# The second mixer's channel products by Strassen's seven block products, on a float32 attention and two-mixer kernel

## The chip, the cores and the metric

The kernel runs on one core of one Trainium2 chip. The metric is the time of one execution on the device in microseconds (us), the median of several executions; lower is better.

## What is computed

Clustered attention (a query sees the keys whose nearest centroid is its own), then two mixers on the result, all in float32. The part that matters here is the second mixer, and in it the channel part, the last two lines:

```python
def _moe2_ref(x, w_tok1, w_tok2, w_ch1, w_ch2) -> np.ndarray:
    xt = x.transpose(0, 2, 1)
    h = np.maximum(xt @ w_tok1, 0.0) @ w_tok2
    u = x + h.transpose(0, 2, 1)
    h2 = np.maximum(u @ w_ch1, 0.0) @ w_ch2
    return (u + h2).astype(np.float32)
```

Here x is 2 batches of 768 tokens by 512 channels, the token part goes through 256 columns, the channel part through 1536. The first mixer has the same channel part with 2048 columns. Weights arrive as 64-bit floats.

## The kernel before

TensorE runs float32 products in its fp32r form, which keeps fewer bits than float32. So every factor is split in two, a rounded high part and the rest, and each product takes three matmuls: high by high, high by low, low by high. A helper `mm` on line 73 issues every matmul of the products, so all have this line; `rnd` (L78, ScalarE) makes a high part, `sub` (L85, VectorE or GpSimd) the low part.

The program is written out by hand in Python loops, so every engine executes exactly the order in which the code records its instructions. It has four stretches.

1. Attention: 96 tile steps. ScalarE, VectorE and TensorE work in turn.
2. The first mixer's channel part. Tokens go in 3 passes of 512 columns (2 batches of 768 tokens make 1536), hidden columns in 16 blocks of 128, so 48 units. A unit is `hidden` (12 matmuls of 512 columns into bank 4 or 5), its eviction `hidden_out` (ScalarE takes the ReLU as `gh`, then VectorE makes `gl`), and `outmm` (12 matmuls of 512 columns into banks 0 to 3). The generator `half_slots` alternates them: `hidden(k+1)`, then `outmm(k)`. Each 12 matmuls are called a half slot here; 96 of them make this stretch.
3. The second mixer's token part, `tok(b)` for each batch: 6 times 4 transposes (L874), 36 matmuls of 512 columns, 48 of 384, in 20 pieces, of which one goes between two half slots.
4. The second mixer's channel part: the same `hidden` and `outmm` over 3 passes and 12 blocks, 36 units.

Beside the half slots runs the conversion of the weights from 64 bits (`conv`: one ScalarE instruction, L96, then four on VectorE, L100, L103, L106, L109), the split in high and low (L78, and L85 on GpSimd), and a write to a DRAM scratch (`scr_a` for the first mixer, `scr_b` for the second). The second mixer's weights go through it in 24 blocks of 512 columns, one every second half slot from the 40th on (`narrow`, `tick`). In the third pass of the first mixer and in the whole of the second, `feed` loads each unit's weights back from the scratch, two transfers of 512 KB per unit, into three rotating buffers; they are asked for some two units ahead. All of these transfers are issued by SyncE, in program order, to one hardware queue.

VectorE also adds the residual back together (L796, high plus low part), once per pass and mixer, and adds the products to it (L801).

## Time and profile before

| | |
|---|---|
| median of 3 runs | 752.43 us (751.09 to 754.22) |
| span of the profiled execution | 754.4 us |
| TensorE busy | 742.3 us (98%), 3902 matmuls recorded |
| VectorE busy | 467.4 us (62%) |
| ScalarE busy | 312.8 us (41%) |
| GpSimd busy | 169.8 us (23%) |
| TensorE clock granted, mean | 0.997 of full speed |

The profile was taken of one execution. For that execution the page gives the span from the first to the last instruction and no separate time; the span lies 0.2 us above the longest of the three runs. Matmuls overlap in the pipeline, so how long one costs is read from the distance between starts of neighbours, not from its duration.

### The profile page before, as it was taken

To read this page: it belongs to the slowest core of one execution; us is meant where nothing else is said; L and a number is where in the kernel's file an instruction comes from. 1 tells how busy PE (TensorE), PEld (TensorE's weight loads), DVE (VectorE), ACT (ScalarE), POOL (GpSimd) and SP (SyncE) were. 2 spreads that over 40 slices of the span, in tenths; PEclk is the share of its full clock that TensorE was granted. 3 is DMA by queue.
4 is the path that set the end of the run, shared out by engine and by line. 5 is a ranking of instruction groups with operands and counts; after the bars stand their busy time and mean duration, and the time that the engine had idled before them with its cause. 6 is when DMAs were issued, how large, how long until landed. Compare 5 with 4: busy or idle time off the path is not lost.

```text
span 754.4 us, 10584 instructions
## 1 busy us (share of the span) xinstructions
PE 742.3 (98%) x3902; PEld 589.3 (78%) x3902; DVE 467.4 (62%) x695; ACT 312.8 (41%) x568; POOL 169.8 (23%) x149
## 2 busy tenths in 40 slices
...
GB/s 179 189 195 220 139 190 214 220 209 131 71 37 124 121 181 195 215 201 189 177 111 128 245 369 358 314 238 280 260 318 204 201 113 293 194 190 206 238 190 84
DMA packets 51555, 149.60 MB, mean 198 GB/s; under 512 B 7696, under 2 KB 15760, under 8 KB 49456
## 3 DMA queue, kind: packets, MB, share of 16 engines
...
q14 instruction: 20, 0.16, 0.1%
...
## 4 chain that ended last, share of the span: by engine, by line
PE 94%; DMA 1%; DVE 1%; ACT 1%; SPq 1%; issue 0%; POOL 0%; ACTq 0%; POOLq 0%; DVEq 0%
PE ps L73 83%; PE ps L319 8%; DMA qk<-pt 1%; DMA sq__81<-in_qT_dram 1%; PE ps L874 1%; PE ps L382 1%; PE ps L339 1%; PE ps L405 0%; ACT p L302 0%; DVE nm L297 0%; POOL qk L85 0%; SPq L257 0%; SPq L268 0%; ACT pt L78 0%; DVE am L219 0%
## 5 line engine op out<-in xcount | busy, mean ns | idle before, releaser
L778 DVE SCALAR_TENSOR_TENSOR gl<-ps,gh 128x512 fp32r<-128x512 f32 x84 | 58.0, 691 | 209.6 <-ACT gh L777 209.6
L777 ACT ACTIVATE gh<-ps 128x512 fp32r<-128x512 f32 x84 | 50.2, 598 | 312.8 <-PE ps L73 312.8
L73 PE MATMUL ps<-gh,qk 128*128 128x512 f32 x544 | 179.6, 391 | 0.1
L73 PEld LDWEIGHTS ps<-gh,qk 128*128 128x128 f32 x544 | 102.1, 188 | 21.6 <-issue 0.5
L73 PE MATMUL ps<-qk 112*128 112x384 f32 (+2 forms) x456 | 109.7, 367 | 5.3 <-ACT p L302 4.0
L297 DVE TENSOR_REDUCE nm<-ps 128x1 f32<-128x768 f32 x96 | 91.2, 954 | 30.6 <-PE ps L73 29.3
L73 PE MATMUL ps<-gl,qk 128*128 128x512 f32 x272 | 106.0, 390 | 0.0
L85 POOL TENSOR_TENSOR qk<-c__77,qk 128x512 fp32r<-128x512 f32 x40 | 54.9, 1380 | 190.7 <-ACT qk L78 162.8
L302 ACT ACTIVATE p<-ps,nm 128x768 f32<-128x768 f32 x96 | 86.1, 899 | 22.8 <-DVE nm L297 20.7
L319 PEld LDWEIGHTS ps<-ident,p 128*128 128x128 f32 x576 | 69.1, 142 | 32.8 <-issue 26.9
L319 PE MATMUL ps<-ident,p 128*128 128x128 f32 x576 | 91.9, 279 | 0.4 <-DVE pt L324 0.3
L73 PEld LDWEIGHTS ps<-qk 112*128 112x128 f32 (+1 forms) x456 | 76.9, 191 | 13.5 <-ACT p L302 7.6
L73 PE MATMUL ps<-u2h,qk 128*128 128x512 f32 x224 | 73.9, 391 | 0.0
L73 PE MATMUL ps<-pt,vr 128*64 128x384 f32 x384 | 72.1, 498 | 0.0
L326 ACT COPY pt<-ps 128x512 f32<-128x512 f32 x96 | 55.7, 586 | 28.0 <-PE ps L319 25.1
L73 PEld LDWEIGHTS ps<-gl,qk 128*128 128x128 f32 x272 | 51.1, 188 | 10.2
L73 PE MATMUL ps<-u1h,qk 128*128 128x512 f32 x160 | 52.6, 390 | 0.0
L73 PEld LDWEIGHTS ps<-u2h,qk 128*128 128x128 f32 x224 | 42.1, 188 | 8.6
L100 DVE TENSOR_SCALAR c__77<-c__77 128x512 f32<-128x512 f32 (+2 forms) x47 | 47.7, 1015 | 0.8 <-ACT c__77 L96 0.7
L109 DVE SCALAR_TENSOR_TENSOR c__77<-c__76,c__77 128x512 int32<-128x512 int32 (+2 forms) x47 | 43.4, 924 | 1.5
L106 DVE SCALAR_TENSOR_TENSOR c__77<-c__76,c__77 128x512 int32<-128x512 int32 (+2 forms) x47 | 43.5, 925 | 1.1
L73 PE MATMUL ps<-u2l,qk 128*128 128x512 f32 x112 | 43.6, 390 | 0.0
...
## 6 DMA issues: line engine op xcount, KB each, us to landing
qk<-scr_b SPq DMA_DIRECT2D x72, 512.0 KB, 4.2
...
qk<-scr_a SPq DMA_DIRECT2D x32, 512.0 KB, 7.4
c__76<-in_wb_dram SPq DMA_DIRECT2D x24, 512.0 KB, 5.3
scr_b<-qk SPq DMA_DIRECT2D x24, 512.0 KB, 5.0
scr_a<-wx SPq DMA_DIRECT2D x16, 512.0 KB, 3.3
scr_a<-qk SPq DMA_DIRECT2D x16, 512.0 KB, 3.2
...
```

The lines of the kernel that those rows point to most:

```text
L73: pe.matmul(o, lhsT=l, rhs=r, start=start, stop=stop, **kw)
L85: eng.tensor_tensor(out=o, in0=a, in1=b, op=ALU.subtract)
L100: dve.tensor_scalar(out=dst, in0=dst, scalar1=2.0 ** -15, scalar2=122879.9921875, op0=ALU.max, op1=ALU.min)
L106: dve.scalar_tensor_tensor(out=d, in0=lo, scalar=29, in1=d, op0=ALU.logical_shift_right, op1=ALU.bitwise_or)
L109: dve.scalar_tensor_tensor(out=d, in0=hi, scalar=-0x40000000, in1=d, op0=ALU.bitwise_and, op1=ALU.bitwise_or)
L297: dve.tensor_reduce(out=nm[:, n % 4 : n % 4 + 1], in_=ps[:, b0 : b0 + 2, 0:HS], axis=AX.XY, op=ALU.max, negate=True)
L302: act.activation(p32[n % NP32].rearrange("p (j k) -> p j k", j=2), ps[:, b0 : b0 + 2, 0:HS], AF.Exp, bias=nm[:, n % 4 : n % 4 + 1], accum_ ...
L319: pe.transpose(ps[:, tb[j], ts(i, P)], p32[n % NP32][:, ts(c, P)], ident)
L326: act.copy(o, ps[:, tb[j], :])
L339: pe.transpose(ps[:, bk, ts(t, P)], osb[q % 2][:, ts(t, P)], ident)
L777: act.activation(gh, o, AF.Relu)
L778: dve.scalar_tensor_tensor(out=gl, in0=o, scalar=0.0, in1=f32(gh), op0=ALU.max, op1=ALU.subtract)
```

## The change

The last stretch is rewritten by the method of Strassen (in Winograd's form, which shares sums). A product of two matrices cut in 2 by 2 blocks needs seven block products in place of eight, if sums of the blocks are formed first and sums of the products afterwards. Both channel products of the second mixer are done so. For the first, tokens of a batch are halved (384 each), channels are halved, and two hidden blocks form a pair; for the second likewise.

- Weight sums: `quad` takes the place of `narrow` for these weights. One quad converts 1024 columns (two hidden blocks, one of the two weights), forms the four sums on VectorE, splits seven blocks of 256 columns (VectorE now subtracts for four of them, GpSimd for three) and writes 3584 columns to `scr_b` by two transfers, 768 KB and 1024 KB. There are 12, placed by the table `line` at half slots 54 to 92, with steps from four before to three after.
- Token sums: `build_u` forms the seven operands of a batch from the mixer's input, in tiles of 768 columns.
- Products: `h_mm` is one of the seven for the first weight, 6 matmuls of 384 columns, `h_out` its eviction and the sums and ReLUs that come after it; `o_mm` is one of the seven for the second weight, for one half of its rows, also 6 matmuls of 384 columns, `o_out` its addition to the result. A run is a batch and two pairs: 14 products of each kind. In the loop the products of the next run's first weight alternate with those of this run's second weight; those of the first run alternate with the pieces of `tok(1)`.
- Buffers: `turn_over` gives the conversion's buffers up for a ring of weights at half slot 93. `load1` and `load2` fetch weights by 256 to 1024 KB.
- The residual: `umm_out` lets ScalarE copy the transposed input back to `xn`, and the additions on L796 are gone.

```diff
-    scr = {0: dp.tile([NFA, 2, P, 1024], F32, name="scr_a"), 1: dp.tile([NFB, 2, P, 1024], F32, name="scr_b")}
+    NPR = NFB // 2
+    scr = dp.tile([NFA, 2, P, 1024], F32, name="scr_a")
+    scr2 = dp.tile([NPR, 2, P, 7 * 512], F32, name="scr_b")
...
-        return [lambda: rnd(act, uh, o), lambda: sub(dve, ul, o, f32(uh))]
+        return [lambda: rnd(act, uh, o), lambda: sub(dve, ul, o, f32(uh)), lambda: act.copy(xn[:, b, :, t, :], o)]
...
+    def quad(q, d, n):
+
+        pr, w = divmod(q, 2)
+        r64, r32 = w64[n % 2], w32[n % 2]
+        ops = conv(r32, r64)
+        r = r32.rearrange("p (i n) -> p i n", n=256)
+        i12 = 1 + w
+        r11, r12, r21, r22 = r[:, 0, :], r[:, i12, :], r[:, 3 - i12, :], r[:, 3, :]
+        A, B = stA[2 if q == 2 * NPR - 1 else q % 2], stB[q % 2]
+        raw_, hi_ = s32, f32(B[:, :, 0, :])
+        if d == 1:
+            raw_load(r64.rearrange("p (f n) -> p f n", f=2), wb[2 * pr : 2 * pr + 2, :, ts(w, 512)].rearrange("f p n -> p f n"))
+        elif d < 6:
+            ops[{3: 0, 4: 1, 4.5: 2, 5: 3, 5.5: 4}[d]]()
+        elif d == 6:
+            sub(dve, raw_[:, 3, :], r11, r21)
+            sub(dve, raw_[:, 1, :], r22, raw_[:, 3, :])
+            sub(dve, raw_[:, 2, :], r12, raw_[:, 1, :])
+            dve.scalar_tensor_tensor(out=raw_[:, 0, :], in0=r21, scalar=-1.0, in1=r22, op0=ALU.mult, op1=ALU.subtract)
+        elif d == 7:
+            rnd(act, A[:, 0, 0, :], r11)
+            rnd(act, A[:, 1:3, 0, :], r[:, i12 : 4 : 3 - i12, :])
+            rnd(act, B[:, :, 0, :], raw_)
+            sub(pool, A[:, 0, 1, :], r11, f32(A[:, 0, 0, :]))
+            sub(pool, A[:, 1:3, 1, :], r[:, i12 : 4 : 3 - i12, :], f32(A[:, 1:3, 0, :]))
+        elif d == 7.5:
+            sub(dve, B[:, :, 1, :], raw_, hi_)
+        elif d == 8:
+            sp.dma_start(scr2[pr, w, :, 0:1536], f32(A).rearrange("p i h n -> p (i h n)"))
+            sp.dma_start(scr2[pr, w, :, 1536:3584], f32(B).rearrange("p i h n -> p (i h n)"))
...
-        uh, ul = fst["u"][p]
-        if lo == 0 and f == hi - 3:
-
-            for b, s, n, k in pieces(p * TW, TW):
-                for c in range(NC):
-                    dve.tensor_tensor(out=x2[b][:, c, s : s + n], in0=f32(uh[:, c, k : k + n]), in1=f32(ul[:, c, k : k + n]), op=ALU.add)
...
+    line = [(wide, 6, 10), (wide, 7, 15), (wide, 8, 17), (wide, 9, 20), (wide, 10, 23), (wide, 11, 26), (wide, 12, 29), (mixer, 0, 33),
+            (wide, 13, 37), (wide, 14, 40), (wide, 15, 43), (mixer, 1, 46), (mixer, 2, 48), (mixer, 3, 50)]
+    line += [(quad, q, h) for q, h in enumerate((54, 59, 62, 65, 69, 72, 75, 79, 82, 85, 89, 92))]
+    for n, (f, k, h) in enumerate(line, 6):
+        steps = [(h - 4, (3,)), (h - 3, (4, 4.5)), (h - 2, (5, 5.5))]
+        if f is quad:
+            steps += [(h - 1, (6,)), (h, (7,)), (h + 1, (7.5,)), (h + 3, (8,))]
+        else:
+            steps += [(h, (6, 6.5)), (h + 1, (7,))]
+        if n > 7:
+            steps.append((line[n - 8][2] - 1, (1,)))
+        for s, ds in steps:
...
+    ORDER = (1, 5, 6, 3, 7, 2, 4)
+    PLACE = (0, 3, 4, 5, 6, 1, 2)
+    CHUNKS = ((0, 1), (1, 2), (3, 2), (5, 2))
+    HB = ((4, 5), (0, 1))
+    OB2 = ((2, 3), (6, 7))
+    NG = NPR // 2
+    CHAIN = (0, 1, 0, 1, 0, 1, 0)
+    FRESH = (True, True, False, False, False, True, False)
...
+    def build_u(b):
+
+        B = {(i, j): x2[b][:, 2 * i : 2 * i + 2, ts(j, HS)] for i in range(2) for j in range(2)}
+        o = {i: ops_u[b][pos(i)] for i in ORDER}
+        hi = lambda i: o[i][:, 0]
+        lo = lambda i: o[i][:, 1]
+
+        def flat(i, x):
+            return [lambda: rnd(act, hi(i), x), lambda: sub(pool, lo(i), x, f32(hi(i)))]
+
+        t = [fz[:, 768 * i : 768 * i + 768].rearrange("p (c n) -> p c n", c=2) for i in range(2)]
+
+        def cut(i, x, eng=pool):
+            return [lambda: rnd(act, hi(i), x), lambda: sub(eng, lo(i), x, f32(hi(i)))]
+
+        def add(o, x, y, op):
+            return [lambda: dve.tensor_tensor(out=o, in0=x, in1=y, op=op)]
+
+        return (flat(1, B[0, 0]) + add(t[0], B[0, 0], B[0, 1], ALU.subtract) + cut(5, t[0], dve) + add(t[1], B[1, 1], t[0], ALU.add)
+                + cut(6, t[1], dve) + add(t[0], B[1, 0], t[1], ALU.subtract) + flat(3, B[1, 1])
+                + add(t[1], B[1, 1], B[0, 1], ALU.subtract) + cut(7, t[1]) + flat(2, B[1, 0]) + cut(4, t[0], dve))
+
...
+    def turn_over():
+
+        cp_ctx.close()
+        op = ctx.enter_context(tc.tile_pool(name="op", bufs=1, side="right"))
+        ring_ = op.tile([P, 4096], F32R, name="ring")
+        mid_ = op.tile([P, 5 * HS], F32, name="mid")
+        w1b.extend([ring_[:, ts(i, 1024)] for i in range(4)] + [wx_[:, 3072:4096]])
+        tmps.extend([mid_[:, ts(i, HS)] for i in range(5)] + [fz[:, 1536 + HS * i : 1536 + HS * i + HS] for i in range(2)])
+
...
+    runs = [(b, k) for b in range(NB) for k in range(NG)]
+    seq1 = [(b, 2 * k + i, c) for b, k in runs for i in range(2) for c in range(4)]
+    seq2 = [(b, k, c) for b, k in runs for c in range(4)]
+    at1, at2 = {}, {}
+
+    def load1(n):
+        if n < len(seq1):
+            b, pr, c = seq1[n]
+            s, m = CHUNKS[c]
+            x = w1b[n % len(w1b)][:, 0 : 512 * m]
+            sp.dma_start(f32(x), scr2[pr, 0, :, 512 * PLACE[s] : 512 * (PLACE[s] + m)])
+            for i in range(m):
+                at1[b, pr, s + i] = x[:, ts(i, 512)].rearrange("p (h n) -> p h n", h=2), n, i == m - 1
+
+    def load2(n):
+        if n < len(seq2):
+            b, k, c = seq2[n]
+            s, m = CHUNKS[c]
+            x = w2b[n % len(w2b)][:, 0 : 1024 * m].rearrange("p (r n) -> p r n", r=2)
+            sp.dma_start(f32(x), scr2[2 * k : 2 * k + 2, 1, :, 512 * PLACE[s] : 512 * (PLACE[s] + m)].rearrange("r p n -> p r n"))
+            for i in range(m):
+                at2[b, k, s + i] = x[:, :, ts(i, 512)].rearrange("p r (h n) -> p r h n", h=2), n, i == m - 1
+
...
+    def h_mm(b, pr, s):
+        w, n, ends = at1[b, pr, s]
+        u = ops_u[b][s]
+        o, on = ps[:, HB[pr % 2][CHAIN[s]], 0:HS], dict(skip_group_check=not FRESH[s])
+        for c in range(2):
+            cs = ts(c, P)
+            mm(o, w[:, 0, cs], u[:, 0, c, :], c == 0 and FRESH[s], False, **on)
+            mm(o, w[:, 0, cs], u[:, 1, c, :], False, False, **on)
+            mm(o, w[:, 1, cs], u[:, 0, c, :], False, c == 1, **on)
+        if ends:
+            load1(n + len(w1b))
+
+    def h_out(b, pr, s):
+        x = ps[:, HB[pr % 2][CHAIN[s]], 0:HS]
+        g = gs.setdefault((b, pr), {})
+        hi, lo = (lambda i: g[i][:, 0, :]), (lambda i: g[i][:, 1, :])
...
+        if s == 0:
+            held_[1] = tmp()
+            act.copy(held_[1], x)
+        elif s == 1:
+            held_[3] = tmp()
+            act.copy(held_[3], x)
+        elif s == 2:
+            held_[0] = tmp()
+            act.copy(held_[0], x)
+        elif s == 3:
+            dve.tensor_tensor(out=held_[0], in0=x, in1=held_[0], op=ALU.add)
+            act.activation(held_[0], held_[0], AF.Relu)
+        elif s == 4:
+            new(3, 7)
+            held_[7] = tmp()
+            dve.tensor_tensor(out=held_[3], in0=x, in1=held_[3], op=ALU.add)
+            top(3, held_[3])
+            relu_less(held_[7], held_[3], held_[0], ALU.subtract)
+            cut(7, held_[7])
...
+    def o_mm(b, k, s, j):
+        w, n, ends = at2[b, k, s]
+        o, on = ps[:, OB2[j][CHAIN[s]], 0:HS], dict(skip_group_check=not FRESH[s])
+        for i in range(2):
+            g = gs[b, 2 * k + i][ORDER[s]]
+            wh, wl = (w[:, i, h, ts(j, P)] for h in range(2))
+            mm(o, wh, g[:, 0, :], i == 0 and FRESH[s], False, **on)
+            mm(o, wh, g[:, 1, :], False, False, **on)
+            mm(o, wl, g[:, 0, :], False, i == 1, **on)
+        if j:
+            gfree.extend(gs[b, 2 * k + i].pop(ORDER[s]) for i in range(2))
+            if ends:
+                load2(n + len(w2b))
+
...
-    while done < end(0, 2) - 24:
+    while done < 68:
         for t in bg:
             next(t, None)
         advance(done + 1)
-    drain(tok(0), end(0, 2) - 2)
-    advance(end(0, 2))
-    drain(tok(1), end(1, 0) - 2)
-    for _ in gen:
+    drain(tok(0), END - 2)
+    todo = build_u(0)
+    while done < END:
+        next(bg[1], None)
+        for _ in range(3):
+            if todo:
+                todo.pop(0)()
+        if done == END - 3:
+            for t in bg:
+                for _ in t:
+                    pass
+            turn_over()
+            for n in range(len(w1b)):
+                load1(n)
+        advance(done + 1)
+    for f in todo:
+        f()
+
+    t = tok(1)
+    for i in range(14):
+        pr, s = divmod(i, 7)
+        h_mm(0, pr, s)
+        h_out(0, pr, s)
+        for _ in range(1 + (1 <= i < 9) if i else 0):
+            next(t, None)
+        if i == 9:
+            load2(0)
+    for _ in t:
         pass
+    for n in range(1, len(w2b)):
+        load2(n)
+    todo = []
+    for r, (b, k) in enumerate(runs):
+        nxt = runs[r + 1] if r + 1 < len(runs) else None
+        if (b, k) == (0, 0):
+            todo = build_u(1)
+        for i in range(14):
+            if nxt:
+                pr, s = divmod(i, 7)
+                pr += 2 * nxt[1]
+                h_mm(nxt[0], pr, s)
+            s_, j = divmod(i, 2)
+            o_mm(b, k, s_, j)
+            if nxt:
+                for x in {6: (), 7: (6, 7)}.get(i, (i,)):
+                    h_out(nxt[0], 2 * nxt[1] + x // 7, x % 7)
+            o_out(b, k, s_, j)
+            send(2 if nxt else 0)
+            for _ in range(int(r == 0 and 4 < i) + 2 * int(r == 1 and i > 7)):
+                if todo and (r == 1 or len(todo) > 9):
+                    todo.pop(0)()
+    send(0)
```

Three places in the order of instructions follow. The first is SyncE's queue in the third pass of the first mixer, before (c is the conversion's buffer, qk the weights' buffer, scr_a and scr_b the scratches):

```order
L593 DMA scr_b<-qk_73 128x1024
L574 DMA c__76<-in_wb_dram 128x512
L757 DMA qk_73<-scr_a 128x1024
L757 DMA qk_72<-scr_a 128x1024
L593 DMA scr_b<-qk_73 128x1024
L574 DMA c__76<-in_wb_dram 128x512
L757 DMA qk_73<-scr_a 128x1024 x2
```

and the same pass now (c holds two blocks per transfer):

```order
L617 DMA scr_b<-vz 128x1536
L618 DMA scr_b<-qk 128x2048
L766 DMA qk<-scr_a 128x1024 x3
L617 DMA scr_b<-qk 128x1536
L618 DMA scr_b<-qk 128x2048
L535 DMA c__77<-in_wb_dram 128x2x512
L766 DMA qk<-scr_a 128x1024 x3
L535 DMA c__77<-in_wb_dram 128x2x512
L766 DMA qk<-scr_a 128x1024
```

A write of 512 KB ahead of every two weight loads has become a pair of writes of 1792 KB ahead of every three or four.

The second is VectorE in that pass, between the evictions `gl` of two units, before:

```order
L778 SCALAR_TENSOR_TENSOR gl_2308<-ps,gh_2306 128x512
L100 TENSOR_SCALAR c__77<-c__77 128x512
L103 TENSOR_SCALAR c__77<-c__77 128x512
L106 SCALAR_TENSOR_TENSOR c__77<-c__76,c__77 128x512
L109 SCALAR_TENSOR_TENSOR c__77<-c__76,c__77 128x512
L778 SCALAR_TENSOR_TENSOR gl_2309<-ps,gh_2307 128x512
```

and now (the eviction is L787, its output lies in the tile ug; fz holds the sums):

```order
L787 SCALAR_TENSOR_TENSOR ug<-ps,ug 128x512
L100 TENSOR_SCALAR c__78<-c__78 128x1024
L103 TENSOR_SCALAR c__78<-c__78 128x1024
L85 TENSOR_TENSOR qk<-fz,qk 128x4x256
L106 SCALAR_TENSOR_TENSOR c__78<-c__77,c__78 128x1024
L109 SCALAR_TENSOR_TENSOR c__78<-c__77,c__78 128x1024
L787 SCALAR_TENSOR_TENSOR ug<-ps,ug 128x512
L85 TENSOR_TENSOR fz<-c__78 128x256
L85 TENSOR_TENSOR fz<-c__78,fz 128x256 x2
L607 SCALAR_TENSOR_TENSOR fz<-c__78 128x256
```

Between two evictions stand twice the columns, and instructions of a new kind, the sums and a subtraction of 1024 columns.

The third is TensorE where the second mixer's channel part begins, now (ring and wx hold weights; u, wx, qk and vz the token sums; L878 are transposes of `tok(1)`, its matmuls read ug and tt):

```order
L73 MATMUL ps<-u_2310,ring 128x384 x12
L878 MATMUL ps<-ident,xn 128x128 x8
L73 MATMUL ps<-u_2310,ring 128x384 x6
L878 MATMUL ps<-ident,xn 128x128 x8
L73 MATMUL ps<-wx,ring 128x384 x6
L878 MATMUL ps<-ident,xn 128x128 x8
L73 MATMUL ps<-wx,ring 128x384 x6
L73 MATMUL ps<-ug,tt 128x512 x12
L73 MATMUL ps<-qk,ring 128x384 x6
```

Before, a piece of `tok(1)` stood between two half slots of 12 matmuls; here two pieces stand between two products of 6.

## Rows read from the trace of the kernel before

**Rows 1.** The page's head.

```profile
span 754.4 us, 10584 instructions
```

**Rows 2.** Stretches: length, busy us (instructions) PE, PEld, DVE, ACT, POOL; clock, DMA share, GB/s.

```profile
200.00:230.00 30.00, 30.00 (x200) 21.98 (x197) 24.55 (x36) 23.18 (x46) 3.18 (x3) 1.00 0.26 80
230.00:425.00 195.00, 195.00 (x953) 157.80 (x952) 132.33 (x188) 67.91 (x106) 45.22 (x34) 1.00 0.45 162
425.00:475.00 50.00, 49.89 (x232) 40.93 (x231) 38.12 (x57) 16.64 (x30) 10.45 (x9) 1.00 0.98 358
475.00:525.00 50.00, 50.00 (x231) 42.64 (x230) 30.27 (x42) 15.91 (x32) 17.21 (x16) 1.00 0.79 266
```

**Rows 3.** The chain that ended last, from 230 us on, by line.

```profile
by line: PE ps L73 96.6%; PE ps L874 1.0%; PE ps L319 0.9%; PE ps L382 0.7%; PE ps L339 0.2%; DVE xn L801 0.1%; issue 0.0%
```

**Rows 4.** TensorE's timeline, 512- and 384-column matmuls: start us, us, what.

```profile
494.24 0.39 PE L73 MATMUL ps<-gl,qk 128*128 128x512 f32 x1
...
494.92 0.39 PE L73 MATMUL ps<-gl,qk 128*128 128x512 f32 x1
...
496.05 0.33 PE L73 MATMUL ps<-t2h,yh 128*128 128x384 f32 x1
...
496.57 0.35 PE L73 MATMUL ps<-t2h,yh 128*128 128x384 f32 x1
...
497.12 0.39 PE L73 MATMUL ps<-u2h,qk 128*128 128x512 f32 x1
...
499.88 0.33 PE L73 MATMUL ps<-t2h,yh 128*128 128x384 f32 x1
```

**Rows 5.** Weight loads of the same matmuls: start us, us, what.

```profile
496.05 0.19 PEld L73 LDWEIGHTS ps<-t2h,yl 128*128 128x128 f32 x1
496.23 0.19 PEld L73 LDWEIGHTS ps<-t2l,yh 128*128 128x128 f32 x1
```

**Rows 6.** All weight loads of that kind, and the token part's transposes: busy us, mean ns.

```profile
L73 PEld LDWEIGHTS ps<-t2h,yh 128*128 128x128 f32 x32 | 6.0, 188 | 0.6
...
L874 PE MATMUL ps<-ident,xn 128*128 128x128 f32 x48 | 7.2, 272 | 0.0
```

**Rows 7.** VectorE from 230 us on, by shape: busy us, mean ns.

```profile
L778 DVE SCALAR_TENSOR_TENSOR gl<-ps,gh 128x512 fp32r<-128x512 f32 x84 | 58.0, 691 | 209.6 <-ACT gh L777 209.6
L100 DVE TENSOR_SCALAR c__77<-c__77 128x512 f32<-128x512 f32 x27 | 31.4, 1162 | 0.0
...
L106 DVE SCALAR_TENSOR_TENSOR c__77<-c__76,c__77 128x1024 int32<-128x1024 int32 x12 | 15.6, 1297 | 0.0
...
L109 DVE SCALAR_TENSOR_TENSOR c__77<-c__76,c__77 128x1024 int32<-128x1024 int32 x12 | 14.7, 1225 | 0.4
...
L103 DVE TENSOR_SCALAR c__77<-c__77 128x1024 int32<-128x1024 int32 x12 | 12.2, 1017 | 0.4
...
L100 DVE TENSOR_SCALAR c__77<-c__77 128x1024 f32<-128x1024 f32 x12 | 9.0, 752 | 0.8 <-ACT c__77 L96 0.7
...
L796 DVE TENSOR_TENSOR xn<-u1h,u1l 128x256 f32<-128x256 f32 x16 | 7.7, 554 | 0.0
```

**Rows 8.** Line 106, 256 to 376 us, 1024 columns alone: ns min/median/max.

```profile
L106 DVE SCALAR_TENSOR_TENSOR c__77<-c__76,c__77 x11: 1212/1215/2195, 262.1 to 368.7; 128x1024 int32<-128x1024 int32 x11
```

**Rows 9.** GpSimd's subtraction and ScalarE's eviction of 512 columns: busy us, mean ns.

```profile
L85 POOL TENSOR_TENSOR qk<-c__77,qk 128x512 fp32r<-128x512 f32 x38 | 52.3, 1385 | 175.4 <-ACT qk L78 147.6 <-issue 16.8 <-PE ps L73 11.0
...
L875 ACT CAST wx<-ps 128x512 fp32r<-128x512 f32 x12 | 7.0, 585 | 9.7 <-PE ps L874 9.7
```

**Rows 10.** DMA, 400 to 425 us: issues, KB each, us to landing.

```profile
c__76<-in_wb_dram SPq DMA_DIRECT2D x4, 512.0 KB, 4.2
```

**Rows 11.** DMA, 425 to 450 us: all bytes, then issues as above.

```profile
DMA packets 2428, 8.86 MB, mean 354 GB/s; under 512 B 270, under 2 KB 270, under 8 KB 2426
...
scr_b<-qk SPq DMA_DIRECT2D x5, 512.0 KB, 7.7
```

**Rows 12.** The fullest five us of it, columns as in rows 2.

```profile
440.00:445.00 5.00, 5.00 (x24) 4.14 (x23) 3.63 (x5) 1.24 (x4) 1.29 (x1) 1.00 1.00 384
```

221 lines of the change are left out of this document (123 added, 98 removed).

## Prediction

> **What bounds the kernel now.** I read the head of the page [rows 1], then the stretches one by one, because the shares of the whole span mix the attention with the rest. From 230 us on TensorE is busy in every microsecond, at the full clock (1.00, so 2.4 GHz), while VectorE has 132 of 195 us to do and the DMA engines move 162 GB/s [rows 2]. The chain of waits says the same: 96.6% of what ended last is `mm` on TensorE [rows 3]. So from there on time is matmuls times their spacing, and an edit elsewhere costs nothing until it makes TensorE wait. One stretch stands out: from 425 to 475 us the DMA engines are at 0.98 of their capacity, and TensorE idles 0.11 us, next to nothing [rows 2]. Transfers do queue up there: a 512 KB transfer of the conversion lands 4.2 us after its issue before 425 us, 7.7 us after [rows 10, 11]. The weight loads are asked for long enough ahead to hide that.
>
> **The spacing of matmuls.** Three 512-column matmuls in the row start 494.92 - 494.24 = 0.68 us apart, 0.227 each [rows 4]. Six 384-column ones of the token part take 497.12 - 496.05 = 1.07, 0.178 each. Two bounds stand in the same rows. The first three take 0.52, 0.173 each. And the twelve 512s behind the six are slowed: 499.88 - 496.05 = 3.83 us, less 12 x 0.227 = 2.72, leaves 1.11, 0.185 each, if what the short ones borrow is paid back later.
>
> **The change, part by part.** I sum against the profiled span, 754.4, which is 2.0 above the median of 752.4, and take the difference off the median.
>
> *Products.* Removed: 36 units of 24 matmuls, 864 x 0.227 = 195.9 us. Added: 2 batches x 6 pairs x 7 products x 6 = 504 for the first weight, 2 batches x 3 runs x 14 x 6 = 504 for the second, 1008 x 0.178 = 179.4. That is -16.5. Columns fall by an eighth, time by 8%, since each matmul has a part that does not shrink. Bounds: 1008 x 0.173 = 174.4 (-21.5) and 1008 x 0.185 = 186.5 (-9.4). I take the six in a row, the nearest to a long stream.
>
> The rows show a small fixed part: 128 columns more cost 0.049 us, so about 0.03 of the 0.178 does not scale. The Trainium skill speaks against the change here: its page "TensorE: Matmul & The Clock Gate" (section "Back-to-back issue gap") has the spacing set by the weight load as well as the matmul, and gives 81 ns at 128 columns and 131 ns at 512. On a straight line between them 384 columns would be 114 ns, an estimate from that page, and 1008 of them 115 us against 113 for 864: no gain. The trace disagrees with these figures (227 ns at 512), so the sum goes by the rows.
>
> *Conversion and writes, half slots 51 to 96.* Here the change adds work beside a TensorE that must not wait. The time of the cover: 45 half slots of 2.72 are 122.4 us, plus `tok(0)`: 36 x 0.227 + 48 x 0.178 + half of the transposes' 7.2 us [rows 6] = 20.3. Together 142.7.
>
> VectorE: per quad the four conversion instructions of 1024 columns cost 0.75 + 1.02 + 1.30 + 1.23 = 4.29 [rows 7]. The four sums of 256 columns are like L796, 0.55 each, 2.2. The subtraction of 1024 columns does not occur; twice an eviction of 512 bounds it at 1.4, two conversion instructions of that size cost 1.2, I take 1.2. That is 7.7, and 12 quads 92.4. Beside them 22 evictions `gl` at 0.69 are 15.2, the 16 evictions of `tok(0)` at no more than that 11.1, the residual of a pass 8 x 0.55 = 4.4, `build_u` 7 instructions of 768 columns at about 1.2 (three times 256, less the fixed part), 8.6. Sum 131.7 of 142.7, 92%. It fits on average, but it comes in pieces of 1 to 2 us that stand ahead of a `gl`, which has to be done some 5.4 us (two half slots) after its product.
>
> And these prices are not firm: L106 takes 1.22 us in the median and up to 2.20 [rows 8], L100 1.16 at 512 columns where it needs 0.75 at 1024 [rows 7]. The short form is the one that runs while GpSimd subtracts for 1.39 us [rows 9]. The Trainium skill's page "SBUF — State Buffer" (section "Who interferes with whom") states the cause: VectorE in some forms, and with two inputs in SBUF, shares a port with GpSimd, and one waits for the other's whole instruction. The rows agree with that. The new sums and the subtraction all have two inputs in SBUF. If two instructions per quad wait 1 us each, the sum is 155.7, 13 us over.
>
> Transfers, half slots 59 to 96, where the first mixer's last pass loads its weights (37 x 2.72 + 20.3 = 121 us of TensorE): 32 loads of 0.52 MB are 16.8 MB, 8 raw loads of 1.05 MB 8.4, 11 quads written at 1.84 MB 20.2, the first loads of the new ring 2.1: 47.5 MB, 393 GB/s. Before, the queue moved 354 GB/s over 25 us [rows 11] and 384 in its best five [rows 12]. That makes 134 or 124 us, 13 or 3 over. Part of an excess is swallowed, as loads are asked for ahead and the last writes may end late. But the writes now come as 1.8 MB (5 us) in one piece ahead of the weight loads in SyncE's queue, and near half slot 68 a quad's write and a raw load stand there together, 2.9 MB or 8 us. The two excesses are not added: a TensorE that waits for the one gives the other time. Taking 0 to 13, I put 6, nearer to the smaller excess.
>
> *Turn-over and first run.* `turn_over` lets the first ring load queue behind the last two quads' writes (3.7 MB, 10 us, of which three half slots, 8.2, are covered): 0 to 2. In the first run two transposing pieces of `tok(1)` stand between two products of 1.07 us; their two banks come free after a ScalarE copy of 0.59 [rows 9] and a VectorE subtraction of 0.69, some 1.5 with the hand-overs, against 1.07 + 0.3. A few tenths three times, about 1 us before the first product of `tok(1)`, which waits for the queue of these evictions, and its ReLU eviction. Sum 3, between 0 and 6. Before, 12 matmuls hid all that.
>
> *Residual.* 32 additions on L796 go, 16 of which alone are 7.7 us of VectorE [rows 7]; from 230 us on VectorE was not the bound, so 0. ScalarE's copies: 8 of 12 lie beside half slots and are hidden by them; four fall in the attention, where ScalarE is busy 23 of 30 us [rows 2]; at 0.59 each 0 to 2.4, I take 0.5, since a quarter of its time is free.
>
> *The last stretch's evictions.* A run has 28 products, 30 us; its VectorE work is 14 additions and 20 other evictions at no more than 0.69, 23.5; between two uses of a bank lie three products, 3.2 us, so 0. Weights are 44 MB in 180 us, 245 GB/s, under what moves now: 0.
>
> Sum: -16.5 + 6 + 3 + 0.5 = -7.0. From 752.4 that is **745.4**.
>
> **The rivals.**
>
> *The stage hides it all.* Transfers reach 384 GB/s and VectorE stays at 92%. For it: the kernel carried 0.98 of DMA share without a wait [rows 2]. Then -16.5 + 2 = -14.5: 738, at best spacing 733.
>
> *Weight load sets the pace.* A load is put at 188 ns [rows 6], and one starts 0.18 after the other [rows 5]. In a stream of 1008 with nothing long between, at 188 each, the products take 189.5: -6.4 + 9.5 = +3.1, 755.5. Against it: the loads in rows 5 already overlap. The skill's page on TensorE, named above, points this way. This is also how the change could fail to do what it says.
>
> *VectorE becomes the bound (slower).* If L100 costs in 1024 columns twice what it does in 512 (2.3) and one more instruction waits 1 us, a quad is 10.2, 12 are 122, the sum 162 of 142.7: 19 over. Then -16.5 + 19 + 3.5 = +6: 758.5. It turns to a loss by 0.5% when a quad costs over 10 us. For it: L100's mean in rows 7. Against it: the 1024-column forms have paid this seldom, and GpSimd now has 768 columns per quad in place of 1024.
>
> **How the numbers follow.** A measurement of this kernel cannot tell less than 0.5% (3.8 us) from no change. Forecast (-3.8 to -12) 0.47, all hidden 0.19, weight load 0.12, VectorE 0.13; 0.09 for mixtures between forecast and no change. Weight load and mixtures fall mostly within 0.5%: faster 0.66, same 0.18, slower 0.16. The range, 738 to 757, leaves out the best spacing and the far end of the VectorE case; the forecast's own is 740 to 749.
>
> **What would show it.** Right: in the last stretch 384-column matmuls 0.178 apart without gaps; in half slots 60 to 75 TensorE gaps that sum to a few us, released by DMA (scr_a loads) or by the `gl` eviction; landing times of scr_a loads over 9 us there; 1 us pieces of waiting in the first run. Wrong: spacing of 0.185 or more, or no gaps at all before the last stretch, or VectorE without a pause from half slot 54 on and TensorE waiting for `gl` each unit.

## The result, and the profile after

The changed kernel takes 756.56 us in the median (754.48 to 759.53, 10 runs), the kernel before 752.87 beside it (750.84 to 755.50): a ratio of 1.0052, 95% interval 1.0035 to 1.0070. By the ratio that is 3.9 us slower, where 7.0 us faster was forecast. The profiled execution took 757.82, its span is 756.0. The spans of the two profiles, 754.4 and 756.0, lie closer together, since the profiled execution of before lost time in the attention: at 61 us TensorE waited 2.36 us, with a granted clock of 0.93 from 50 to 75 us, and the changed kernel's did not. So times are compared by the ratio.

First the stretches, with the columns of [rows 2]: length, busy us (instructions) of PE, PEld, DVE, ACT and POOL, granted clock, DMA share, GB/s. 475 to 547.4 ends at the first product of the second mixer's channel part; the last two lie in it.

```profile
230.00:425.00 195.00, 195.00 (x945) 158.33 (x944) 141.24 (x183) 76.93 (x113) 54.10 (x39) 1.00 0.50 182
425.00:475.00 50.00, 45.32 (x196) 36.57 (x195) 38.11 (x56) 18.91 (x29) 9.63 (x8) 0.93 1.00 392
475.00:547.40 72.40, 66.67 (x294) 55.77 (x293) 60.58 (x73) 24.70 (x36) 22.46 (x14) 0.95 0.87 338
565.00:636.00 71.00, 70.24 (x395) 68.91 (x395) 48.92 (x81) 26.86 (x53) 23.57 (x19) 1.00 0.70 241
636.00:671.00 35.00, 32.46 (x177) 32.14 (x176) 24.12 (x38) 13.38 (x26) 13.10 (x10) 0.95 0.67 226
```

From 230 to 425 us nothing differs for TensorE: it is full. From 425 to 475 it was 49.89 of 50 busy before [rows 2] and is 45.32 now, and its clock, which was 1.00 in every row of [rows 2], is 0.93. The same two signs stand in the next stretch and in 636 to 671. Who ended these waits is in the view of TensorE's waits (what for; us in total, times, longest):

```profile
PE ps L73 <- DVE ug L787: 5.7, 1, 5.7
PE ps L73 <- DVE xn L1150: 4.1, 4, 2.5
PE ps L73 <- ACT qk L78: 2.5, 1, 2.5
PE ps L73 <- DMA qk<-scr_a: 2.1, 2, 2.0
...
PE ps L73 <- DVE ug L85: 0.5, 1, 0.5
```

From 230 us on these are four waits of 2 us and more, and the view names VectorE for two of them, ScalarE for one and a load for one. Where they lie, by TensorE's timeline (start us, us, what; at the end the idle time before and its releaser), and at the end a piece of the quiet stream of products:

```profile
432.02 4.24 PE L73 MATMUL ps<-ug,qk 128*128 128x512 f32 x11 [2.54 <-ACT qk L78]
...
454.81 4.59 PE L73 MATMUL ps<-ug,qk 128*128 128x512 f32 x12 [1.97 <-DMA qk<-scr_a]
...
540.05 7.54 PE L73 MATMUL ps<-ug,qk 128*128 128x512 f32 x23 [5.73 <-DVE ug L787]
...
646.79 2.29 PE L73 MATMUL ps<-qk,tt 128*128 128x384 f32 x6 [2.54 <-DVE xn L1150]
...
690.68 1.23 PE L73 MATMUL ps<-qk,tt 128*128 128x384 f32 x6
...
693.85 1.21 PE L73 MATMUL ps<-ug,ring 128*128 128x384 f32 x6
```

The last two rows have 18 products between them: 3.17 / 18 = 0.176 us each, beside 0.178 in [rows 4]. So the products give what they were said to give, 1008 x 0.176 = 177.4 for 195.9, 18.5 us less. The first four rows show that a wait costs more than itself: 6 products take 2.29 us behind the wait at 644, and 1.23 in the quiet stream; 12 matmuls of 512 columns take 4.59 at 455, where 0.227 each [rows 4] would be 2.7. The clock says why, in stretches of 10 us:

```profile
420.00:430.00 10.00, 9.48 (x42) 7.51 (x40) 9.86 (x16) 2.55 (x5) 3.36 (x4) 1.00 0.96 366
430.00:440.00 10.00, 7.98 (x31) 6.55 (x32) 6.72 (x11) 3.25 (x5) 0.76 (x1) 0.83 1.02 419
...
450.00:460.00 10.00, 8.04 (x33) 6.30 (x32) 7.48 (x11) 4.26 (x8) 2.43 (x2) 0.83 1.00 377
...
520.00:530.00 10.00, 10.00 (x45) 8.14 (x44) 9.97 (x10) 5.40 (x9) 5.06 (x4) 1.00 0.95 391
530.00:540.00 10.00, 4.32 (x20) 3.23 (x18) 9.90 (x11) 2.42 (x5) 5.37 (x3) 0.88 0.67 243
540.00:550.00 10.00, 9.95 (x40) 8.47 (x41) 6.24 (x7) 3.06 (x6) 4.90 (x2) 0.78 0.82 292
```

The clock has two levels, 1.2 and 2.4 GHz, so 0.83 over 10 us is 3.4 us at the lower one. The four low rows make 3.4 + 3.4 + 2.4 + 4.4 = 13.6 us at half rate. Of these 2.4 lie inside the wait that ends at 540.05 (the clock is 0.50 from 538 us on, while TensorE stands still) and cost nothing; the other 11.2 cost up to 5.6 us. The waits themselves are 10.2. Together 15.8 us in the conversion's stretch, where the prediction had 6.

**What the three waits there are made of.** The first two are for weights that land late. For the one at 429 the view names ScalarE's rounding (L78), but that only ended at the same moment: the trace's semaphores have a `scr_a` load, asked for at 420.41 us, land at 431.89, and TensorE's next weight load starts at 431.99, before L78 ends at 432.03. In e2, e3, e7 and e13 a wait stands at the same place, and the view names a `scr_a` load in all four. Ahead of this load SyncE had issued, from 418.17 us on, a raw load, another `scr_a` load and a quad's two writes, 3.4 MB, or 8 us at 419 GB/s. ScalarE's timeline shows the same queue: it stands still until a quad's blocks have left the staging buffer (the write of the quad two before), and the ReLU of the next unit, L786, is queued behind. TensorE does not wait for this ReLU, which starts at 432.95:

```profile
428.25 0.94 ACT L78 ACTIVATE qk<-c__78 128x256 fp32r<-128x256 f32 x2 [3.52 <-DMA scr_b<-qk]
430.97 1.06 ACT L78 ACTIVATE qk<-fz 128x1024 fp32r<-128x1024 f32 x1 [1.77 <-DMA scr_b<-qk]
...
432.95 0.57 ACT L786 ACTIVATE ug<-ps 128x512 fp32r<-128x512 f32 x1
```

The DMA view of 425 to 450 us (all bytes; then KB each and us from issue to landing) answers to [rows 11]: the bytes went from 8.86 to 10.47 MB, the rate from 354 to 419 GB/s, and a landing takes some 14 us.

```profile
DMA packets 2201, 10.47 MB, mean 419 GB/s; under 512 B 217, under 2 KB 217, under 8 KB 1814
...
qk<-scr_a SPq DMA_DIRECT2D x7, 512.0 KB, 14.2
...
scr_b<-qk SPq DMA_DIRECT2D x2, 1024.0 KB, 13.6
```

Before, the same view has for these loads:

```profile
qk<-scr_a SPq DMA_DIRECT2D x9, 512.0 KB, 8.3
```

The one at 534 is VectorE's. It is busy 9.97 and 9.90 of 10 us in the rows above, and its timeline shows what stands between two evictions `gl` (L787): conversion, the sums of a quad, and `build_u(0)` on 768 columns, several of them long while GpSimd subtracts (its rows, in a fence of their own).

```profile
530.84 2.75 DVE L109 SCALAR_TENSOR_TENSOR c__78<-c__77,c__78 128x1024 int32<-128x1024 int32 x1
533.52 0.95 DVE L85 TENSOR_TENSOR u<-fz,u 128x768 fp32r<-128x768 f32 x1
534.39 1.47 DVE L1008 TENSOR_TENSOR fz<-xn,fz 128x768 f32<-128x768 f32 x1
535.78 1.48 DVE L85 TENSOR_TENSOR fz<-c__78 128x256 f32<-128x256 f32 x1
...
539.30 0.69 DVE L787 SCALAR_TENSOR_TENSOR ug<-ps,ug 128x512 fp32r<-128x512 f32 x1
```

```profile
529.63 2.88 POOL L85 TENSOR_TENSOR wx<-xn,wx 128x768 fp32r<-128x768 f32 x1 [4.71 <-ACT wx L78]
534.13 2.86 POOL L85 TENSOR_TENSOR tt<-c__78,tt 128x256 fp32r<-128x256 f32 x2 [1.61 <-DMA scr_b<-qk]
```

L109 takes 2.75 us beside GpSimd's subtraction; its mean was 1.23 before [rows 7]. The Trainium skill's page "SBUF — State Buffer" (section "Who interferes with whom") has a VectorE instruction with two SBUF inputs contend with a GpSimd instruction that reads SBUF; this row agrees.

### The profile page after: what moved, and what is told of

It reads as the page before. It is cut to its first block, busy times and chain, and to the rows that moved or that the text cites. A ratio compares the mean times of both kernels' runs of the same rounds, so it can differ in the third digit from the quotient of the medians.

```text
span 756.0 us, 11118 instructions
## 1 busy us (share of the span) xinstructions
PE 730.5 (97%) x4046; PEld 606.9 (80%) x4046; DVE 565.1 (75%) x829; ACT 371.9 (49%) x660; POOL 221.9 (29%) x181
## 4 chain that ended last, share of the span: by engine, by line
PE 85%; DVE 8%; DMA 5%; issue 1%; ACT 1%; POOL 0%; SPq 0%; POOLq 0%; DVEq 0%; ACTq 0%
PE ps L73 74%; PE ps L323 9%; DMA qk<-scr_a 2%; DMA scr_b<-qk 1%; DMA tt<-scr_b 1%; DVE mid L1058 1%; PE ps L386 1%; PE ps L343 1%; DVE qk L1058 1%; DVE fz L1008 1%; DVE c__78 L109 1%; PE ps L409 0%; DMA qk<-p 0%; DVE fz L85 0%; DVE ug L85 0%
## 5 line engine op out<-in xcount | busy, mean ns | idle before, releaser
L73 PE MATMUL ps<-ug,qk 128*128 128x512 f32 x576 | 143.7, 402 | 10.4 <-DVE ug L787 5.7
L73 PEld LDWEIGHTS ps<-ug,qk 128*128 128x128 f32 x576 | 111.0, 194 | 34.8 <-DVE ug L787 6.4
L73 PE MATMUL ps<-qk,tt 128*128 128x384 f32 (+1 forms) x528 | 107.9, 344 | 4.4 <-DVE xn L1150 4.1
L73 PEld LDWEIGHTS ps<-qk,tt 128*128 128x128 f32 x528 | 94.6, 189 | 7.9 <-DVE xn L1150 6.4
L786 ACT ACTIVATE ug<-ps 128x512 fp32r<-128x512 f32 x48 | 28.6, 596 | 114.7 <-PE ps L73 109.8
L1150 DVE TENSOR_TENSOR xn<-ps,xn 128x384 f32<-128x384 f32 x84 | 46.0, 553 | 39.0 <-PE ps L73 38.8
L787 DVE SCALAR_TENSOR_TENSOR ug<-ps,ug 128x512 fp32r<-128x512 f32 x48 | 33.1, 689 | 54.1 <-ACT ug L786 54.0
L85 POOL TENSOR_TENSOR qk<-mid,qk 128x384 fp32r<-128x384 f32 x36 | 41.5, 1161 | 107.8 <-ACT qk L78 94.5
L85 POOL TENSOR_TENSOR qk<-c__78,qk 128x512 fp32r<-128x512 f32 (+1 forms) x26 | 33.9, 1323 | 128.1 <-ACT qk L78 111.8
L106 DVE SCALAR_TENSOR_TENSOR c__78<-c__77,c__78 128x1024 int32<-128x1024 int32 (+2 forms) x32 | 42.9, 1341 | 0.2
L109 DVE SCALAR_TENSOR_TENSOR c__78<-c__77,c__78 128x1024 int32<-128x1024 int32 (+2 forms) x32 | 41.6, 1299 | 1.0
L96 ACT ACTIVATE c__78<-c__77 128x1024 f32<-128x1024 f32 (+2 forms) x32 | 35.5, 1110 | 12.5 <-DMA c__77<-in_wb_dram 6.0
```

Source lines behind the costliest of these rows:

```text
L73: pe.matmul(o, lhsT=l, rhs=r, start=start, stop=stop, **kw)
L85: eng.tensor_tensor(out=o, in0=a, in1=b, op=ALU.subtract)
L96: act.activation(dst, hi.bitcast(F32), AF.Abs)
L106: dve.scalar_tensor_tensor(out=d, in0=lo, scalar=29, in1=d, op0=ALU.logical_shift_right, op1=ALU.bitwise_or)
L109: dve.scalar_tensor_tensor(out=d, in0=hi, scalar=-0x40000000, in1=d, op0=ALU.bitwise_and, op1=ALU.bitwise_or)
L786: act.activation(gh, o, AF.Relu)
```

## The experiments

Theory A: the queue of transfers holds TensorE up, through ScalarE and the weight loads. Theory B: VectorE does. Theory C, for the clock: a TensorE that has waited long enough goes on at half rate, so that a wait is paid again. The rival to all: the products or the last stretch give less than counted. Each timed run has the kernel before beside it; 1.0052 is the changed kernel's ratio.

**e1, fewer bytes written.**

```diff
-            sp.dma_start(scr2[pr, w, :, 1536:3584], f32(B).rearrange("p i h n -> p (i h n)"))
...
-    PLACE = (0, 3, 4, 5, 6, 1, 2)
+    PLACE = (0, 0, 0, 1, 1, 1, 1)
```

> Each quad writes only its three own blocks (0.79 MB of 1.84), and the ring reads every product's weights from that part, so that the products' values are not those of the reference; the number and size of the reads, and all work on the engines, stay as in the changed kernel. Theory A (the written bytes hold up ScalarE and the weight loads): the TensorE waits at 429 us (2.7) and 452 us (2.1) go, and with them the two half-rate spells of 3.4 us behind them (1.7 each), about -8 us: 748 to 749 against 756.6. Waits at 534 us (5.9) and 644 us (2.7) stay. Theory B (VectorE is what holds TensorE up): nothing changes by more than 2 us, 755 to 757.

Measured: 748.83, ratio 0.9965 (0.9948 to 0.9982), 7.7 below the changed kernel (6.5 by the two ratios). From 425 to 475 us TensorE is busy 49.66 of 50 at the full clock; the wait for `gl` (now L786) has the same length to the hundredth. First its windows, then its timeline:

```profile
425.00:475.00 50.00, 49.66 (x231) 40.83 (x230) 39.81 (x62) 20.73 (x32) 8.87 (x8) 1.00 0.96 360
475.00:537.90 62.90, 57.17 (x251) 47.84 (x250) 54.79 (x64) 22.69 (x34) 22.43 (x14) 0.95 0.66 240
```

```profile
530.30 2.93 PE L73 MATMUL ps<-ug,qk 128*128 128x512 f32 x6 [5.73 <-DVE ug L786]
```

Theory A holds for the first two waits, by way of the weight loads, and only for them. The DMA engines are at 0.66 in the second stretch, and the third wait is as long as ever, so it does not come from the queue.

**e2, build_u spread out.**

```diff
-        for _ in range(3):
+        for _ in range(2):
             if todo:
...
-            for _ in range(int(r == 0 and 4 < i) + 2 * int(r == 1 and i > 7)):
+            for _ in range(int(r == 0 and 4 < i) + int(r == 1 and i > 3)):
```

> The factors of the first weight (build_u) are issued two instead of three instructions per half slot for batch 0, one instead of two per product for batch 1, from an earlier product on; nothing is left out. Theory B (768-column instructions of VectorE and GpSimd in one place ahead of the evictions): the waits at 534 us (5.9 us and a half-rate spell that costs 3.4) and 644 us (2.7 and 1.7) go, less 1 to 2 us for the last factors that now end after the last unit: -11 to -13, 744 to 746. Theory A (the writes of the last quads hold up the end of the conversion): the wait at 534 stays over 4 us, and only 644 goes: about 752. Waits at 429 and 452 stay by both.

Measured: 757.78, ratio 1.0057 (1.0037 to 1.0078): no gain. In this kernel three factors of batch 0 are replaced before their last products read them, and the products then wait for GpSimd and ScalarE (625 to 631 us). It tells nothing clean of the wait at 644; e7 repeats it in another order.

**e3, no sums on VectorE.**

```diff
-            sub(dve, raw_[:, 3, :], r11, r21)
-            sub(dve, raw_[:, 1, :], r22, raw_[:, 3, :])
...
+            pass
```

> The four sums of the weights' blocks on VectorE are left out (the four plain blocks are rounded in their place, so the products' values are not those of the reference): 48 instructions and some 21 us of VectorE less, in half slots 53 to 91; transfers, ScalarE and GpSimd as in the changed kernel. Theory A: the waits at 429 (2.7) and 452 (2.1) stay, the one at 534 loses no more than the two sums that stand there; 753 to 756. Theory B: VectorE's room takes most of the waits before 540 us away, 10 to 16 us with their half-rate spells; 741 to 746.

Measured: 752.48, ratio 0.9996 (0.9982 to 1.0010), 4.1 below the changed kernel: between the two theories. Its timeline has the early waits where A has them, released by late weights (5.4 us in three), and two thirds of the one at 534 (2.44 and 1.25 in place of 5.73).

```profile
430.10 5.69 PE L73 MATMUL ps<-ug,qk 128*128 128x512 f32 x24 [2.32 <-DMA qk<-scr_a]
...
532.68 3.01 PE L73 MATMUL ps<-ug,qk 128*128 128x512 f32 x12 [2.44 <-DVE ug L784]
536.94 2.83 PE L73 MATMUL ps<-ug,qk 128*128 128x512 f32 x11 [1.25 <-DVE ug L784]
```

24 matmuls in 5.69 us is the full rate: two waits of 2.3 and 2.4 us here were followed by no spell at all, which theory C must explain. This is the profile of one execution, 750.24, among the fastest; over the ten the mean granted clock goes from 0.991 to 0.998.

**e4, four quads of twelve.**

```diff
-    line += [(quad, q, h) for q, h in enumerate((54, 59, 62, 65, 69, 72, 75, 79, 82, 85, 89, 92))]
+    line += [(quad, q, h) for q, h in enumerate((54, 62, 70, 80))]
...
-            sp.dma_start(f32(x), scr2[pr, 0, :, 512 * PLACE[s] : 512 * (PLACE[s] + m)])
+            sp.dma_start(f32(x), scr2[pr % 2, 0, :, 512 * PLACE[s] : 512 * (PLACE[s] + m)])
```

> Only four of the twelve quads are converted and written, at half slots 54, 62, 70 and 80, and every product reads weights of these four (values not those of the reference); TensorE's instructions, and the reads of the last stretch, are all there. It shows what the seven products give when the conversion costs TensorE nothing. Both theories: the waits at 429 and 452 go; the wait at 534 keeps only what build_u makes, 0 to 3 us; 644 stays (2.7 and 1.7). The sum of the prediction without its term for the conversion, with the measured spacing of 0.175 (-19.2) and with the residual copy: 737 to 741. Rival (the seven products themselves give less than counted, through waits of the last stretch on evictions and weights): over 745, with the stretch from the last eviction of the units to the end at over 212 us as in the changed kernel.

Measured: 741.05, ratio 0.9839 (0.9808 to 0.9869). With the same products and the same reads behind them, TensorE does not wait from 390 us to the first product:

```profile
425.00:475.00 50.00, 50.00 (x234) 41.38 (x233) 22.57 (x36) 12.40 (x20) 1.99 (x2) 1.00 0.70 256
475.00:531.90 56.90, 56.90 (x262) 48.30 (x261) 24.06 (x33) 12.41 (x19) 10.74 (x6) 1.00 0.52 181
...
620.00:655.00 35.00, 32.47 (x177) 32.15 (x176) 24.02 (x38) 13.40 (x26) 13.11 (x10) 0.95 0.68 225
```

The rival is out: the products give their gain. The price of the eight quads left out is what lies between the two ratios, (1.0052 - 0.9839) x 752 = 16.0 us, give or take 2.7; four quads cost no wait. `build_u(0)` alone, three instructions per half slot, makes no wait. The wait of 2.5 us in the last stretch, with its clock of 0.95, is still here, so it has nothing to do with the conversion.

**e5, the residual alone, in the kernel before.**

```diff
-        return [lambda: rnd(act, uh, o), lambda: sub(dve, ul, o, f32(uh))]
+        return [lambda: rnd(act, uh, o), lambda: sub(dve, ul, o, f32(uh)), lambda: act.copy(xn[:, b, :, t, :], o)]
...
-        if lo == 0 and f == hi - 3:
+        if m and lo == 0 and f == hi - 3:
```

> The kernel before with one part of the change alone: the residual of the first mixer is copied by ScalarE from PSUM, and the 16 additions on VectorE that formed it are gone. By the prediction +0.5 us (four copies in the attention) and nothing for VectorE: within 0.3% of the kernel before, 751 to 754. Rival: ScalarE's copies stand in the attention's chain and cost their bound, +2.4 us: 754 to 755; the start of the first mixer then shows it, since the changed kernel reached it 3.7 us sooner than before's profiled run, not later.

Measured: 752.45 against 752.80, ratio 1.0003 (0.9990 to 1.0015). No effect beyond 1 us, in keeping with the +0.5 predicted.

**e6, three blocks of the first mixer kept in SBUF.**

```diff
-    units += [(0, p, f) for p in range(2, NPASS) for f in range(NFA)]
+    KEEP = (14, 15, 13)
+    units += [(0, p, f) for p in range(2, NPASS) for f in (*KEEP, *range(NFA - 3))]
...
-            if u2_ % 2 == 0 and 2 * NFA <= u < K:
+            if u2_ % 2 == 0 and 2 * NFA + 3 <= u < K:
...
-            else:
+            elif k < NFA - 3:
```

> The changed kernel, with the first mixer's last pass begun at the three blocks (14, 15, 13) whose weights are still in SBUF: their six reads (3.1 MB, half slots 60 to 66) and their six writes (3.1 MB, half slots 38 to 44) are gone, all else is as before. Theory A (the queue of transfers is too long where quads are written and weights are read together; by e1 it costs 7 to 8 us): the waits at 429 and 452 us go without a byte less of the quads, 748 to 750. Rival (it is the writes' own length, since ScalarE's rounding of quad q waits for the write of quad q-2, whatever else is in the queue): the wait at 429 stays at over 2 us with its half-rate spell, 754 to 756. The wait at 534 stays by both.

Measured: 752.86, ratio 0.9993 (0.9977 to 1.0009), 3.7 below the changed kernel: between the two again. In place of the waits of 2.5 and 2.0 us stand two, 1.2 for VectorE's additions at the end of a pass (L807) and 1.4 for a `scr_a` load, and nothing runs at half rate before 529. So the queue's length counts, and the rival is out, but 3.1 MB of reads less do not empty it.

**e7, build_u spread out, in order.**

```diff
-            for _ in range(int(r == 0 and 4 < i) + 2 * int(r == 1 and i > 7)):
-                if todo and (r == 1 or len(todo) > 9):
+            for _ in range(int(r == 0 and 4 < i or r == 1 and i > 7 or r == 2 and i < 3)):
+                if todo and (r or len(todo) > 9):
```

(and two per half slot, as in e2)

> As e2, build_u two instructions per half slot for batch 0, but for batch 1 one per product from where its buffers are free, so that nothing is overwritten early and the output is the reference's. Going by e2's profile, in which the waits near 534 us summed to 5.2 in four pieces with one half-rate spell (5.9 and 6.8 us of half rate in the changed kernel): -3 to -4 there. At 644 theory B (the 768-column pieces of VectorE and GpSimd stand ahead of an addition that frees a bank) has the wait of 2.7 and its spell of 3.4 go: -4. Sum -6 to -8, 748 to 751; if the early waits (428 to 454 us) come out as in e2 rather than as in the changed kernel, 2 less or more.

Measured: 752.01, ratio 0.9986 (0.9968 to 1.0003), 4.5 below the changed kernel and a little less than forecast. The wait in the last stretch shrinks from 2.54 to 0.27, and the products behind it run at the full rate (6 in 1.32 us, not 2.29):

```profile
643.55 1.32 PE L73 MATMUL ps<-qk,tt 128*128 128x384 f32 x6 [0.27 <-DVE xn L1150]
```

Near 534 the one wait becomes three, together still 5 us: spreading `build_u` moves it, and does not take it away. The longest of them, 3.17 us before 543.14, has no spell behind it (clock 1.00 from 525 to 555 us).

**e8, both, with earlier quads and earlier loads.**

```diff
-    line += [(quad, q, h) for q, h in enumerate((54, 59, 62, 65, 69, 72, 75, 79, 82, 85, 89, 92))]
+    line += [(quad, q, h) for q, h in enumerate((54, 59, 62, 65, 68, 71, 74, 77, 80, 83, 86, 89))]
...
-            u2_ = n + 4 + (1, -2)[i]
+            u2_ = n + 4 + (1, -1)[i]
```

> Resident blocks (e6), lazy build_u (e7), the second halves of the weights asked for one half slot earlier, and the last nine quads one to three half slots earlier, so that the last is rounded at 89 instead of 92 and build_u(0) meets fewer of its instructions. If the losses are the three named (transfers at 425 to 455 us, build_u(0) at 534, build_u(1) at 644, each with its half-rate spells), they add up and nearly all go: 740 to 744, faster than both kernels by 1% or more. If VectorE as a whole is the limit from half slot 54 to 96 (it is busy 129 of 160 us there in the changed kernel), the earlier quads only move the waits forward: 747 to 751.

Measured: 741.71, ratio 0.9846 (0.9819 to 0.9873): **faster than both kernels**, with the whole change in it. From 475 us to its first product TensorE never waits, with the DMA engines at 0.97 and 383 GB/s:

```profile
475.00:538.80 63.80, 63.80 (x292) 54.01 (x291) 50.30 (x64) 23.73 (x35) 17.95 (x14) 1.00 0.97 383
```

What is left are three waits between 430 and 466 us, 4.7 in all.

**e9, quads in the middle later.** Beside e8:

```diff
-enumerate((54, 59, 62, 65, 68, 71, 74, 77, 80, 83, 86, 89))]
+enumerate((54, 59, 63, 66, 70, 73, 76, 79, 81, 84, 86, 89))]
```

> As e8, but quads 2 to 7 one or two half slots later, 9 to 12 at 81 to 89: e8 left waits at 430 (1.3 us), 440 (1.1) and 463 (2.7 with a half-rate spell, 1.7), the last two released by weights that came late, while its transfers fell to a half afterwards (slices 27 to 30 of 40). If the length of the queue is what is left, the three go: -4 to -6, 736 to 738. If moving quads only moves the waits (VectorE then meets two quads every five half slots near 80 to 89), they come back behind 500 us: 741 to 745.

Measured: 743.16, ratio 0.9883 (0.9848 to 0.9917), not better than e8. The early waits shrink, and waits for `gl` come back at 516 to 534 us: the second case.

**e10, only the edits for VectorE.** Beside e8, the resident blocks (e6) and the earlier loads are taken back:

```diff
-            u2_ = n + 4 + (1, -1)[i]
+            u2_ = n + 4 + (1, -2)[i]
```

> e8 without its two edits of the transfers (blocks resident, weights asked for earlier): only the lazy build_u and the earlier quads. It tells what of e8's gain (15 us against the changed kernel) is VectorE's and what the queue's. By the sums so far (e1: the queue costs 7 to 8; e7: lazy build_u gives 4.5; e8 shows nothing left at 534) the VectorE part is 534 and 644 with their spells, 13: 743 to 745, with waits at 429 and 452 kept. Rival: earlier quads make the queue worse at 430 to 470, where e7 waited 5 us: 747 to 751.

Measured: 744.35, ratio 0.9885 (0.9862 to 0.9908), as forecast. Of e8's gain the queue's two edits are 0.9885 - 0.9846 = 0.4%, 3 us, give or take 2.7; the rest is VectorE's, by order alone.

**e11, extra waits by size.** In the kernel before, with 7 to 16 in the table:

```diff
         act.activation(gh, o, AF.Relu)
+        for _ in range({52: 7, 56: 8, 64: 9, 68: 10, 76: 12, 80: 16}.get(k, 0)):
+            dve.tensor_scalar(out=c32_[:, 0:1024], in0=c32_[:, 0:1024], scalar1=2.0 ** -15, scalar2=122879.9921875, op0=ALU.max, op1=ALU.min)
```

> The kernel before, in its quiet last stretch: 7, 8, 9, 10, 12 and 16 extra instructions of VectorE (0.75 us each on 1024 columns, on data that nobody reads afterwards) ahead of one eviction each (units 52, 56, 64, 68, 76, 80), so that TensorE must wait there. An eviction has some 4.5 us of slack, so the waits should be about 0.7, 1.5, 2.2, 3, 4.5 and 7.5 us, 19 in all. Theory C (a TensorE that has waited 2 us and more goes on at half rate for a while): the granted clock falls behind the waits of 2.2 us and more, by 1.7 us of lost time each (3.4 behind the longest, as at 534 in the changed kernel), 27 in all: 778 to 783. Rival (the half-rate spells come from what else goes on at 430 to 540 us, transfers at the limit and VectorE and GpSimd busy, not from the waits): no spell here, 770 to 773.

Measured: one run, 756.09, span 754.3. Only the sixth place made a wait. In the quiet part VectorE stands idle up to 4.75 us ahead of an eviction, and the extra instructions start in that time: 16 take 11.61 us, 0.73 each, but hold the eviction up by less than 7. The slack behind it is the 4.5 us that was said; the time ahead of it was forgotten (and e14's expectation, with 0.61 and 7.2, reads it no better). The one wait:

```profile
732.55 0.61 PE L73 MATMUL ps<-gl,qk 128*128 128x512 f32 x1 [2.43 <-DVE gl L780]
732.97 1.05 PE L73 MATMUL ps<-gh,qk 128*128 128x512 f32 x2
...
736.54 0.40 PE L73 MATMUL ps<-gh,qk 128*128 128x512 f32 x1
736.77 0.40 PE L73 MATMUL ps<-u2h,qk 128*128 128x512 f32 x1
```

Behind it matmuls start 0.42 apart, then 0.23. The granted clock is 0.78 from 730 to 735 us and 0.88 in the next five, 3.4 us at half rate, so 1.7 us on top of the 2.4. The span is 4.3 us over that of e12, in which nothing waited; these are two single runs, and runs of the kernel before scatter by 2 us and more. This is the quiet end of the old kernel, so neither a full queue (DMA share 0.01 from 730 to 735 us) nor GpSimd is needed for it.

**e12, nine extra instructions at each place.** The table of e11 is now:

```diff
+        for _ in range({52: 9, 56: 9, 64: 9, 68: 9, 76: 9, 80: 9}.get(k, 0)):
```

> As e11 with 9 extra instructions at each of the six places: six waits of about 2.2 us. In e3 waits of 2.5 and 2.6 us were followed by no half-rate spell, in the changed kernel one of 2.1 was. If the size alone decides, all six or none of these are followed by a spell (13 us of waits, and 0 or 10 on top: 766 or 776); if where the wait falls decides too, some are.

Measured: one run, 751.81, span 750.0. No wait, for the reason that e11 gave, and so nothing on its question; it serves as the base.

**e13, earlier quads alone.** The changed kernel with one line of e8:

```diff
-enumerate((54, 59, 62, 65, 69, 72, 75, 79, 82, 85, 89, 92))]
+enumerate((54, 59, 62, 65, 68, 71, 74, 77, 80, 83, 86, 89))]
```

> The changed kernel with nothing but the last nine quads earlier (65, 68, ... 89 in place of 65, 69, ... 92). If the wait of 5.9 us at 534 comes from the meeting of the last quads with build_u(0) on VectorE, it goes with its half-rate spells though build_u is as eager as ever: e10 (744.4) plus the wait at 644 and its spell (2.7 and 1.7), 748 to 749. If build_u's three instructions per half slot were the cause by themselves, 3 us or more stay there: 751 to 754.

Measured: 746.69, ratio 0.9920 (0.9904 to 0.9937), 9.9 below the changed kernel, with one row of numbers. The 5.73 us have become 0.57:

```profile
534.59 2.80 PE L73 MATMUL ps<-ug,qk 128*128 128x512 f32 x11 [0.57 <-DVE ug L787]
```

With e4 this settles the wait at 534: not `build_u(0)` by itself, but its meeting with the last quads in the same half slots. (The last quads at their old places without `build_u(0)` were not run.) TensorE still waits 4.9 us for `scr_a` loads earlier, here with no spell behind them (clock 1.00 from 420 to 630 us), which would account for a gain above the wait at 534 and its spell.

**e14, more extra instructions.**

```diff
+        for _ in range({52: 14, 56: 15, 64: 16, 68: 18, 76: 20, 80: 24}.get(k, 0)):
```

> As e11 with more extra instructions, 14, 15, 16, 18, 20 and 24 at units 52, 56, 64, 68, 76 and 80: e11 showed 0.61 us for one and 7.2 us of slack, so the waits should be about 1.3, 2.0, 2.6, 3.8, 5.0 and 7.4 us, 22 in all (more at the first ones, where VectorE still converts). Theory C: half-rate spells behind those from 2.6 us on, 1.7 us each and 3.4 behind the longest, 8.5: against 750.0, the span of e12, in which nothing waited, 780. Rival (e11's one spell was by chance): under 774.

Measured: one run, 786.27, span 784.5, 34.5 over e12: theory C's side, and over its figure by 4.5. Each of the five visible waits, of 2.4 us and more, has a row of low clock behind it; the last, of some 8 us, has 0.74 over 15 us, more than half of it inside the wait.

**e15, equal waits.**

```diff
+        for _ in range({52: 16, 56: 16, 64: 16, 68: 16, 76: 16, 80: 16}.get(k, 0)):
```

> As e14 with 16 extra instructions at each of the six places: waits of 2.6 us at the last ones, up to 4 at the first. If the size alone decides, a spell stands behind every one of 2.6 us (e11's was): 15.6 of waits or more, and 10 of half rate. If where the wait falls decides too, as e3's 2.5 and 2.6 without a spell suggest, some are without one.

Measured: one run, 776.12, span 774.3, 24.3 over e12. The first two places make waits of 1.4 and 3.9 us, the others four of 2.4 each, alike in releaser and in what is behind them; these four in windows of 11 us:

```profile
649.00:660.00 11.00, 8.56 (x31) 6.57 (x31) 5.47 (x9) 0.60 (x1) 0.00 (x0) 0.84 0.32 104
675.00:686.00 11.00, 8.57 (x38) 6.78 (x37) 5.55 (x9) 0.84 (x2) 0.00 (x0) 1.00 0.40 143
722.00:733.00 11.00, 8.56 (x31) 6.61 (x31) 4.84 (x8) 0.60 (x1) 0.00 (x0) 0.84 0.40 130
748.00:759.00 11.00, 8.56 (x31) 6.58 (x30) 4.94 (x8) 0.60 (x1) 0.00 (x0) 0.84 0.27 90
```

Three are paid again (31 matmuls in the time of 38), the second is not. So the size alone does not decide, and e3's two waits and e7's 3.17 us without a spell are no contradiction. What else does was not varied; that it is the moment at which the wait falls is argued. The Trainium skill's page "TensorE: Matmul & The Clock Gate" (sections "What's actually happening" and "HAM oscillation — how this bites in real kernels") states both: a TensorE that waits between pieces of work goes on at the lower level, and the monitor behind it runs free of the kernel. These rows agree with the first, at shorter waits than those of the page's example, and fit the second without showing it.

## Why the prediction was wrong, step by step

**The products: right.** -16.5 was predicted from 0.178 us; the stream runs at 0.176, -18.5, and e4 shows that the time follows. The rival that weight loads set the pace is out with it: they start as closely as the matmuls, no slower than these rows.

**The conversion and its writes, +6: wrong, 16.0 measured (e4).** This step alone turns the sign: -7.0 + 10 = +3. Its two inputs were good. VectorE was put at 131.7 us, and is busy 29.75 from 390 to 425 us, then 38.11 and 60.58 to the first product, in all 128.4; the transfers were to need 393 GB/s, and move 392 from 425 to 475 us. By themselves the transfers' two waits and their spells make 4.5 + 3.4 = 7.9 us (e1 gave back 6.5 to 7.7), not far from the 6; VectorE's place, put at nothing beside it because 92% fits, made 5.7 + 2.2 = 7.9. What failed is the sentence "The two excesses are not added: a TensorE that waits for the one gives the other time." They lie in different places. The queue is full at 425 to 455 us, VectorE at 520 to 540, and a wait at 430 gives nothing to a collision 100 us later, since the instructions that collide there are tied to half slots, and come later by the same wait. e1 takes the first pair away and leaves 5.73 us of the other; e13 does the reverse. They add: 4.5 and 5.7 us, and with the spells 15.8, beside the 16.0 of e4. A smaller slip: 384 GB/s was the best five us of 425 to 450 only; elsewhere the trace of before has 401 (455 to 460 us) and 419 (695 to 700).

**No term for the clock: the other part of that step.** The sum let a wait cost itself. Here 11.2 us at half rate, up to 5.6 us of time, stand behind 10.2 us of waits in the conversion. e11 shows the same at a place where little else goes on: 2.4 us of wait, about 4 of time.

**Which mechanism.** That a quad's write and a raw load stand together ahead of the weight loads, 8 us of queue, was in the prediction, and the first wait shows just that. And its point that VectorE's work "comes in pieces of 1 to 2 us that stand ahead of a `gl`" was the right one, with too small a size: an average of 92% said 'it fits', where 20 us in a row were at 99 to 100%. What decides there is which instructions share a half slot, as e13 shows.

**The last stretch's evictions, 0: wrong by some 5 us.** The count of a run's VectorE work, 14 additions and 20 evictions, left out `build_u(1)`, which is put into the same products, and it priced every eviction at 0.69 or less. These rows are VectorE's, then GpSimd's, at 641 to 646:

```profile
641.63 2.08 DVE L1058 SCALAR_TENSOR_TENSOR mid<-mid 128x384 f32<-128x384 f32 x1
643.64 2.62 DVE L1058 SCALAR_TENSOR_TENSOR qk<-mid,qk 128x384 fp32r<-128x384 f32 x2
646.19 0.55 DVE L1150 TENSOR_TENSOR xn<-ps,xn 128x384 f32<-128x384 f32 x1
```

```profile
641.14 2.16 POOL L85 TENSOR_TENSOR u<-xn,u 128x768 fp32r<-128x768 f32 x1
```

The addition that frees TensorE's bank (L1150) stands behind sums on two inputs in SBUF (L1058) that take 2.08 us, and 2.62 for two, beside GpSimd's subtractions; the one before them took 0.94. That cost 2.5 us and (0.95 over 35 us) 3.5 us at half rate, 1.7; e7 took it away. Another 1.0 is lost to the last additions, where no next products are left to cover them.

**Turn-over and first run, +3: too much.** The trace has no wait at the turn-over and 0.5 us before the first product of `tok(1)`, where 1 was put; two small waits for L1150, 0.5 in all, come later.

**Residual, +0.5: right within the measurement** (e5, ratio 1.0003).

The sum with measured terms: -18.5 + 16.0 + 1.0 + 4.2 + 1.0 = +3.7; measured +3.9 by the ratio. (The 16.0 is itself a difference from the changed kernel; what is tested is that the other terms make -12.3, where e4 measured -12.1.) Of the rivals, "VectorE becomes the bound" came out with its sign and near its 758.5, but not as it was put (a quad of over 10 us all along): VectorE's 5.7 us in one place, the transfers' 4.5 in another, and the clock on top. So the nearness is luck, and it is luck too that the time lies inside the stated 738 to 757.

What stays open: why just some waits of 2.4 us are followed by the lower clock; and e8's three waits at 430 to 466 us (4.7 us, and 1.7 for a spell) were shortened by e9 at the price of others later.
